# Attention and a maxout FFN on one core: seven visits for three head groups instead of nine, and FFN pieces in the score slots

## The chip, the cores and the metric

One core of one Trainium2 chip. (In this kernel TensorE does the matmuls, VectorE and ScalarE the elementwise work; PSUM is the memory that the matmuls write, and a "piece" or an AV holds banks of it until VectorE or ScalarE has read them.) The metric is the device time of one execution in microseconds (us). Most executions of a kernel agree within 0.3%. Ratios are the mean time of one kernel's fast runs over that of the other's fast runs of the same rounds, so they are not quite the ratios of the medians that stand beside them.

## The reference, cut to what matters

```python
def _attn_ref(q, k, v):                 # 8 batches, 12 heads, 448 tokens, 64 per head
    scores = scale * np.matmul(q, k.transpose(0, 1, 3, 2))
    m = np.max(scores, axis=-1, keepdims=True)
    e = np.exp(scores - m)
    attn = e / (np.sum(e, axis=-1, keepdims=True) + np.exp(-m) + 1e-09)
    return np.matmul(attn, v)

def _moe_ref(x, w1, w2, w3, w_out):     # 3584 tokens, 768 wide
    h = np.maximum(np.maximum(x @ w1, x @ w2), x @ w3)
    return h @ w_out
```

The attention's output, with the heads of a token side by side, is the FFN's `x`.

## The kernel before

The 96 heads are worked in 24 groups of four. A group's scores are seven units. A unit is four matmuls of 64x64 weights and 448 columns ("corners"), one for each quarter of the array, into one slot of two PSUM banks; ScalarE takes the exponential of a slot in one instruction. Then the weighted sum with V ("AV") is done for each of the two pairs of heads: 26 small matmuls (64x64 weights, 65 columns) and 18 wide ones (128x128, 65 columns). TensorE's time between is filled with pieces of the FFN: an up piece is six matmuls of 448 columns into one bank, an output piece six of 384.

The kernel works with eight banks of PSUM: three slots of two, and two single banks for the FFN. An AV takes a slot, so a visit has room for two units and an AV, or three units and no AV: three visits per group.

```python
ps_s = ctx.enter_context(tc.tile_pool(name="ps_s", bufs=3, space=bass.MemoryType.PSUM))
ps_b = ctx.enter_context(tc.tile_pool(name="ps_b", bufs=2, space=bass.MemoryType.PSUM))
...
visits = ((0, 1), (2, 3), (4, 5, 6))
...
for i in range(3, NI):
    ...
    for vi, units in enumerate(visits):
        n = 3 * i + vi
        scores(i, ej, units)                      # corners, then the exponentials
        ...
        if vi < 2:
            finish = av(i - 1, pj, vi, "E" if first else "EO")
        if n in adds:
            add_batch(adds[n])                    # a batch of FFN work becomes available
        per = STEP if first and vi < 2 else share(n)
        if finish:
            one()                                 # one FFN piece, then the rest of the AV
            finish()
        ...
        fill(per)                                 # FFN pieces, banks in turn
```

The last tile of an AV (the 64 tokens that are left of 448 after three tiles of 128, for both heads of the pair) is summed in two banks, so ScalarE copies one half and VectorE adds the other (`finish`): one copy, an add, a reciprocal and two scaled copies for each pair.

The softmax here doesn't subtract the row's maximum and nothing guards it: scores larger than these inputs give would overflow.

Of the kernel before, what the change touches and what calls it, by code (L numbers as in the profile page):

```python
# [17 lines left out]
LAMBDA = 256.0  # L18


@with_exitstack
def kernel(
# [36 lines left out]
    LAST = 6  # L59
# [10 lines left out]
    ps_s = ctx.enter_context(tc.tile_pool(name="ps_s", bufs=3, space=bass.MemoryType.PSUM))  # L70
    ps_b = ctx.enter_context(tc.tile_pool(name="ps_b", bufs=2, space=bass.MemoryType.PSUM))

    ctx.enter_context(tc.manual_schedule())

# [97 lines left out]
    def warm(n, cols=512):  # L172
        ps = ps_b.tile([128, 512], FP32, tag="b", name="warm")
        for _ in range(n):
            nc.tensor.matmul(
                out=ps[:, 0:cols], lhsT=wz[:, 0:128], rhs=wz[:, 0:cols], start=True, stop=True
            )
# [14 lines left out]
    def transpose_pe(i, pr, pool, k_eng, q_engs):  # L192


        def tile_of():
            if pool is ps_s:
                return ps_s.tile([128, 2, 1024], MMDT, tag="s", name="trT")[:, 0]
            return ps_b.tile([128, 1024], MMDT, tag="b", name="trT")

        kr, qr = raw[i]["k"], raw[i]["q"]  # L200
        kj = (0, 1, 2) if pr == 0 else (3, 4, 5, 6)
        qt = (-1, 1, 3, 5, 0, 2, 4) if pr == 0 else (6, 8, 10, 12, 7, 9, 11, 13)
        n = -(-len(qt) // len(q_engs))
        jobs = [(k_eng, "k", kj[0], kr, [2 * b for b in kj])]
        for e, eng in enumerate(q_engs):
            jobs.append((eng, "q", pr * 7 + e * n, qr, qt[e * n : (e + 1) * n]))
        if i not in KT:
            KT[i] = att_pool.tile([P, T * 128], MMDT, tag="KT", name="KT")
            QT[i] = att_pool.tile([P, (NB + 1) * 128], MMDT, tag="QT", name="QT")
        tps = [tile_of() for _ in jobs]  # L210
        for tp, (eng, nm, o, src, toks) in zip(tps, jobs):
            for j, t in enumerate(toks):
                nc.tensor.transpose(
                    out=tp[:, ts(j, 128)],
                    in_=src[:, t + 1 : t + 3, :].rearrange("x t d -> x (t d)"),
                    identity=ident16,
                )
        for tp, (eng, nm, o, src, toks) in zip(tps, jobs):
            dst = {"k": KT, "q": QT}[nm][i]
            evac(eng, dst[:, o * 128 : (o + len(toks)) * 128], tp[:, 0 : len(toks) * 128])  # L220

    def transpose_once(i, nm, eng):
# [4 lines left out]
        tp = ps_b.tile([128, 1024], MMDT, tag="b", name="trT")  # L227
# [62 lines left out]
    def scores(i, ej, units, part="EO"):  # L290
# [5 lines left out]
        for n in range(0, len(units), per):  # L296
            us = units[n : n + per]
            stp = ps_s.tile([128, 2, 512], FP32, tag="s", name="stp")
# [35 lines left out]
    def av_tail(i, ej, pr, ws=(0, 1, 2, 3)):  # L334

        eF, vt = e_buf[ej], vt_buf[i % NV]
        ps = ps_s.tile([128, 2, 512], FP32, tag="s", name="avp")
# [15 lines left out]
    def av_last(i, ej, pr):  # L353



        eF, vx, vt = e_buf[ej], v_buf[i % NV], vt_buf[i % NV]
        ps = avs[i, pr]

        def tile_mm(r, hh, o, rhs, stop):  # L360
            nc.tensor.matmul(  # L361
                out=ps[hh * HP : hh * HP + HP, r, 3 * D1 : 4 * D1],
                lhsT=eF[r * HP : r * HP + HP, o : o + HP],
                rhs=rhs,
                start=False,
                stop=stop,
                skip_group_check=True,
            )

        n = where[pr, None, TL]  # L370
        for hh in range(2):
            tile_mm(hh, hh, e_col(n, 3), vt[hh * HP : hh * HP + HP, pr, 0:D1], False)
        for c, x in enumerate((X1, X3, X2)):
            for r in range(2):
                for hh in range(2):
                    o = e_col(where[pr, hh, x], 3)
                    rhs = vx[r * HP : r * HP + HP, 2 * pr + hh, x[0], 0:D1]
                    tile_mm(r, hh, o, rhs, c == 2)

    def av_main(i, ej, pr, ws=(0, 1, 2, 3), last=False):  # L380
# [29 lines left out]
        if not last:  # L410
            return None
        end = small.tile([P, D1], FP32, tag="end", name="end")
        rl = small.tile([P, 1], FP32, tag="rl", name="rl")
        nc.scalar.activation(out=end, in_=ps[:, 1, 3 * D1 : 4 * D1], func=AF.Copy)  # L414

        def finish():
            nc.vector.tensor_tensor(out=end, in0=ps[:, 0, 3 * D1 : 4 * D1], in1=end, op=ALU.add)
            nc.vector.tensor_scalar(
                out=rl, in0=end[:, D:], scalar1=1.0 / LAMBDA, scalar2=None, op0=ALU.add
            )  # L420
            nc.vector.reciprocal(out=rl, in_=rl)  # L421
            for hh in range(2):
                h = slice(hh * HP, hh * HP + HP)
                nc.scalar.activation(  # L424
                    out=xn[i][0:HP, pr, 3, hh], in_=end[h, 0:D], func=AF.Copy, scale=rl[h]
                )

        return finish
# [14 lines left out]
    def x_transpose_pe(i, part):  # L443
# [3 lines left out]
        tp = ps_b.tile([128, NP, 2, 128], MMDT, tag="b", name="xtp")  # L447
# [10 lines left out]
    def x_transpose_all(i):  # L458
        b, g = groups[i]
        tp = ps_b.tile([128, NP, 4, 128], MMDT, tag="b", name="xtp")  # L460
# [20 lines left out]
    def up_piece(b, fcs, i, q0, qn):  # L481
# [5 lines left out]
        p_i = ps_b.tile([128, 512], FP32, tag="b", name="p_i")  # L487
# [18 lines left out]
    def out_piece(bp, t, c, w, queues):  # L506
# [5 lines left out]
        op_ps = ps_b.tile([128, 512], FP32, tag="b", name="op_ps")  # L512
# [33 lines left out]
    def add_out(b):  # L546
        sy, sc = nc.sync, nc.scalar
        for t in range(0, 3) if b % 2 == 0 else range(3, 7):
            cuts = [(0, NW, None), (NW, NW, (sy, sy))]
            if b == B - 1 and t == 6:  # L550
                cuts = [(0, NW, (sy, sy)), (NW, 256, (sc, sc)), (NW + 256, 128, (sy, sc))]
# [9 lines left out]
    def fill(cols):  # L561
        credit[0] += cols
        while pieces and credit[0] > 0:
            f, a, w = pieces.pop(0)
            f(*a)
            credit[0] -= w
        if not pieces:
            credit[0] = min(credit[0], 0.0)

    def one():  # L570
        if pieces:
            fill(max(0.0, 1.0 - credit[0]))
# [9 lines left out]
    def av(i, ej, pr, part):  # L582
        if i >= LAST:
            av_tail(i, ej, pr, (0, 1, 2))
            av_last(i, ej, pr)
            return av_main(i, ej, pr, (0, 1, 2), True)
# [24 lines left out]
    transpose_pe(0, 0, ps_s, DV, (AC, DV))  # L611
    attend("O", 0, S01)
    transpose_pe(0, 1, ps_b, DV, (DV,))
    attend("O", 0, S23, S46)
    warm(4)
    transpose_pe(1, 0, ps_b, AC, (DV,))
    transpose_pe(1, 1, ps_s, AC, (DV,))
# [5 lines left out]
    transpose_pe(2, 0, ps_b, AC, (DV,))  # L623
    transpose_pe(2, 1, ps_s, AC, (DV,))
# [34 lines left out]
    visits = ((0, 1), (2, 3), (4, 5, 6))  # L659
    adds = {3 * (3 * b + 4) + (b >= PE_X): b for b in range(1, B - 1)}  # L660
# [3 lines left out]
    def share(n):  # L664


        nxt = min([a for a in adds if a > n], default=3 * NI + 2)
        rest = range(n, nxt)
        sums = [AVC if m % 3 < 2 and m < 3 * NI else 0 for m in rest]
# [8 lines left out]
    for i in range(3, NI):  # L678
        ej, pj = (i + 1) % NEB, i % NEB
        first = i == 3  # L680
        if PE_QK <= i + 2 < NI:
            transpose_dma(i + 2)
        if first:
            load_v(i + 2)
        for vi, units in enumerate(visits):
            n = 3 * i + vi
            scores(i, ej, units)
            if i == 4 and vi == 0:
                prep_v(i, DV)
            finish = None  # L690
            if vi < 2:
                finish = av(i - 1, pj, vi, "E" if first else "EO")
            if n in adds:
                add_batch(adds[n])
            per = STEP if first and vi < 2 else share(n)
            if finish:
                one()
                finish()
            if vi == 1 and i > 3 * PE_X:
                x_transpose_dma(i - 1)  # L700
            if vi == 0 and first:
                x_transpose_pe(1, "E")
            if vi == 2 and first:
                x_transpose_pe(i - 1, "E")
                fill(per / 2)
                prep_v(i, DV)
                for w, cols in ((0, (0, NE)), (1, (0, NE)), (2, (NE, NO)), (2, (0, NE))):
                    add_up(0, *cols, [(w, f) for f in (0, 2, 4)])
                add_out(0)
                per = share(n)  # L710
            if vi == 2 and 3 < i <= 3 * PE_X:
                x_transpose_all(i - 1)
            if first:
                fill(per)
                per = 0
            if i + 1 < PE_QK and vi < 2:
                transpose_once(i + 1, "qk"[vi], (AC, DV)[vi])
            fill(per)
        if i + 1 < PE_QK:
            shift_q(i + 1, nc.gpsimd)  # L720
        if first:
            load_qk(i + 3)
        if i < 5:
            load_more(i + 3, i + 4)
        if 5 <= i + 1 < NI:
            prep_v(i + 1, nc.gpsimd)
        if PE_QK <= i + 2 < NI:
            shift_q(i + 2, nc.gpsimd)
        if i >= 5:
            load_more(i + 3, i + 4)  # L730

    for pr in range(NP):
        finish = av(NI - 1, NI % NEB, pr, "EO")
        one()
        finish()
    x_transpose_dma(NI - 1)
# [33 lines left out]
```

## Time and profile before

| | before |
|---|---|
| median of 3 runs | 338.42 us (338.1 to 339.23) |
| span of the profiled run | 336.9 us |
| TensorE, VectorE, ScalarE busy | 97%, 59%, 54% |
| FFN matmul of 448 columns, start to start | 189 ns |
| attention block of a visit with AV (two units) | 1.30 us |
| attention block of a visit without (three units) | 0.69 us |

The busy shares come from the top of the profile's page. The last three rows come from the starts of single matmuls in the trace: the block runs from the first score matmul to the first FFN matmul. TensorE is the bound and hardly waits, so the question is only how many nanoseconds of attention lie between the FFN pieces. The lines that carry this are shown in the prediction.

### The profile page before, as it was taken

To read this page: it belongs to the slowest core of one execution; us is meant where nothing else is said; L and a number is where in the kernel's file an instruction comes from. 1 tells how busy PE (TensorE), PEld (TensorE's weight loads), DVE (VectorE), ACT (ScalarE), POOL (GpSimd) and SP (SyncE) were. 2 spreads that over 40 slices of the span, in tenths; PEclk is the share of its full clock that TensorE was granted. 3 is DMA by queue.
4 is the path that set the end of the run, shared out by engine and by line. 5 is a ranking of instruction groups with operands and counts; after the bars stand their busy time and mean duration, and the time that the engine had idled before them with its cause. 6 is when DMAs were issued, how large, how long until landed. Compare 5 with 4: busy or idle time off the path is not lost.

```text
span 336.9 us, 10248 instructions
## 1 busy us (share of the span) xinstructions
PE 326.1 (97%) x4316; PEld 195.9 (58%) x4316; DVE 199.9 (59%) x521; ACT 183.1 (54%) x289; POOL 146.7 (44%) x260
## 2 busy tenths in 40 slices
PE   7899999999999999999999999999999999999993
PEld 3668788866556655565546646555556555565552
DVE  4556675566566556556656556556556556575552
ACT  4768856655665755676556655666565665420000
POOL 8596578880671539170854328351754000000000
PEclk9999999999999999999999999999999999999999
DMA  8999999799799999969996999989990730124016
GB/s 141 197 200 207 203 205 191 128 161 191 109 108 132 171 234 145 124 96 190 177 156 81 114 259 120 150 99 220 186 149 18 164 89 2 31 47 129 0 33 157
DMA packets 84815, 46.46 MB, mean 138 GB/s; under 512 B 53280, under 2 KB 81312, under 8 KB 84768
## 3 DMA queue, kind: packets, MB, share of 16 engines
q0 software_dynamic: 29120, 21.80, 48.6%
q1 hardware_dynamic: 55264, 23.60, 41.3%
q8 instruction: 34, 0.56, 0.7%
q10 hardware_dynamic: 384, 0.39, 0.4%
q14 instruction: 13, 0.11, 0.1%
HBM read 44.04 MB, written 11.01 MB: 163 GB/s over the span
## 4 chain that ended last, share of the span: by engine, by line
PE 87%; DMA 5%; ACT 2%; DVE 2%; issue 1%; POOL 1%; POOLq 0%; ACTq 0%
PE p_i L490 48%; PE op_ps L514 14%; PE stp L304 11%; PE avp L388 9%; DMA xT<-xn 3%; ACT e L324 2%; DMA ld_q<-in_q_dram 2%; PE avp L344 2%; PE avp L361 1%; DVE xn L404 1%; PE trT L229 1%; DVE QT L190 1%; PE xtp L463 0%; ACT QT L188 0%; DVE rb L401 0%
## 5 line engine op out<-in xcount | busy, mean ns | idle before, releaser
L324 ACT ACTIVATE e<-stp 128x896 f16<-128x896 f32 (+4 forms) x171 | 143.9, 901 | 60.3 <-PE stp L304 60.1
L490 PE MATMUL p_i<-xT,w 128*128 128x448 f16 (+2 forms) x972 | 173.1, 332 | 0.5 <-DMA xT<-xn 0.3
L490 PEld LDWEIGHTS <-w 128*128 128x128 f16 x972 | 90.2, 98 | 69.1 <-issue 6.0
L249 POOL COPY QT<-QT 64x384 f16<-64x384 f16 (+1 forms) x84 | 46.9, 558 | 93.9 <-DMA QT<-ld_q 69.2
L501 DVE TENSOR_TENSOR hT<-hT,p_i 128x448 f16<-128x448 f16 (+2 forms) x96 | 59.7, 622 | 35.7 <-PE p_i L490 35.6
L514 PE MATMUL op_ps<-w,hT 128*128 128x384 f16 (+2 forms) x342 | 58.5, 323 | 0.0
L304 PE MATMUL stp<-QT,KT 64*64 64x448 f16 (+2 forms) x756 | 48.1, 338 | 2.6 <-ACT e L324 0.9
L499 DVE CAST hT<-p_i 128x448 f16<-128x448 f32 (+2 forms) x48 | 30.0, 625 | 25.2 <-PE p_i L490 25.2
L514 PEld LDWEIGHTS <-hT 128*128 128x128 f16 x342 | 32.0, 98 | 22.4 <-issue 2.0
L424 ACT ACTIVATE xn<-end,rl 64x64 f16<-64x64 f32 x72 | 24.9, 346 | 34.5 <-DVE rl L421 34.1
L521 DVE TENSOR_SCALAR o_sb<-op_ps 128x384 f32<-128x384 f32 (+2 forms) x57 | 31.2, 547 | 17.4 <-PE op_ps L514 16.8
L388 PE MATMUL avp<-vx,e 128*128 128x65 f16 x936 | 38.6, 194 | 0.0
L388 PEld LDWEIGHTS <-e 128*128 128x128 f16 x936 | 32.1, 97 | 2.3
L304 PEld LDWEIGHTS <-KT 64*64 64x64 f16 x756 | 15.8, 105 | 26.8 <-issue 23.9
L398 DVE TENSOR_SCALAR rb<-avp 128x6 f32<-128x6 f32 (+2 forms) x54 | 8.8, 164 | 36.8 <-PE avp L388 36.8
L404 DVE TENSOR_TENSOR xn<-avp,rb 128x384 f16<-128x384 f32 (+2 forms) x54 | 29.3, 543 | 1.8
L433 POOL COPY vx<-ld_v 128x768 f16<-128x768 f16 x21 | 17.2, 820 | 6.8 <-issue 4.2
L344 PEld LDWEIGHTS <-e 64*64 64x64 f16 x624 | 13.7, 107 | 8.1 <-issue 1.7
L102 POOL DMA_DIRECT2D ld_q<-in_q_dram x24 | 17.4, 723 | 2.3 <-DMA w<-in_moe_w_dram 1.1
L102 POOL DMA_DIRECT2D ld_k<-in_k_dram x24 | 17.3, 722 | 2.1 <-DMA w<-in_moe_w_out_dram 1.1
L414 ACT ACTIVATE end<-avp 128x65 f32<-128x65 f32 x36 | 8.2, 227 | 17.1 <-PE p_i L490 12.4
L115 POOL DMA_DIRECT2D ld_v<-in_v_dram x24 | 15.2, 634 | 2.6 <-DMA w<-in_moe_w_dram 1.3
(52 smaller groups left out, 162.1 us busy)
## 6 DMA issues: line engine op xcount, KB each, us to landing
out_dram<-o_sb SPq DMA_DIRECT2D x54, 192.0 KB, 4.0
ld_v<-in_v_dram POOLq DMA_DIRECT2D x48, 128.0 KB, 5.1
ld_k<-in_k_dram POOLq DMA_DIRECT2D x23, 224.0 KB, 6.6
ld_q<-in_q_dram POOLq DMA_DIRECT2D x23, 224.0 KB, 7.5
w<-in_moe_w_dram POOLq DMA_DIRECT2D x9, 384.0 KB, 9.2
w<-in_moe_w_out_dram POOLq DMA_DIRECT2D x3, 384.0 KB, 8.5
xT<-xn SPq DMA_TRANSPOSE x18, 4.8
QT<-ld_q SPq DMA_TRANSPOSE x17, 7.3
```

Source lines behind the costliest of these rows:

```text
L102: nc.gpsimd.dma_start(out=tiles[nm][:, 1 : NP * T + 1].rearrange("x (r t) d -> x r (t d)", r=NP)[:, p0:p1], in_=src[:, p0:p1],)
L249: eng.tensor_copy(out=t[d0 : d0 + HP, o * 128 : (o + n) * 128], in_=t[s0 : s0 + HP, a * 128 : (a + n) * 128],)
L304: nc.tensor.matmul(out=stp[half * HP : half * HP + HP, par, j * qn : (j + 1) * qn], lhsT=k_block(i, pr, h2, x[half]), rhs=q_cols(i, pr, h2 ...
L324: nc.scalar.activation(out=dst, in_=src, func=AF.Exp, scale=scale)
L388: nc.tensor.matmul(out=ps[:, hh, j * D1 : (j + 1) * D1], lhsT=eF[:, o : o + 128], rhs=vx[:, 2 * pr + hh, (x[0]), 0:D1], start=False, stop= ...
L404: nc.vector.tensor_tensor(out=xn[i][:, pr, ws[0] : ws[0] + nw].rearrange("p j h d -> p h j d"), in0=acc[:, :, :, 0:D], in1=rb.unsqueeze(3) ...
L424: nc.scalar.activation(out=xn[i][0:HP, pr, 3, hh], in_=end[h, 0:D], func=AF.Copy, scale=rl[h])
L490: nc.tensor.matmul(out=p_i[:, j * qn : (j + 1) * qn], lhsT=w_sb[i][:, dc, ts(fc, 128)], rhs=xT[b][:, dc, q0 : q0 + qn], start=(dc == 0), s ...
L499: nc.vector.tensor_copy(out=dst, in_=src)
L501: nc.vector.tensor_tensor(out=dst, in0=dst, in1=src, op=ALU.max)
L514: nc.tensor.matmul(out=op_ps[:, 0:w], lhsT=hT[bp][:, fc, ts(t, 128)], rhs=wout_sb[:, fc, c : c + w], start=(fc == 0), stop=(fc == NFC - 1),)
L521: nc.vector.tensor_scalar(out=o_sb[:, c : c + w], in0=op_ps[:, 0:w], scalar1=1.0 / LAMBDA, scalar2=None, op0=ALU.mult,)
```

## The change

The intent: three units in every visit, also beside an AV. For that the AV is packed into one bank (7 x 65 = 455 columns of 512) instead of a slot, and its small tiles run in the quarters of the array that a unit's corners leave free: the first unit's two "anti" corners go together with 14 small tiles on the diagonal quarters, and the last unit's diagonal corners with 12 small tiles on the anti ones. Three groups then need seven visits. As the AV holds one of the two single banks, the FFN pieces go into score slots whose exponentials are done, and only the last piece of a visit into the remaining bank. The code makes the second lot of small tiles wait for the first by way of a no-op on ScalarE (the prediction gives the reason). Further, the last tile of an AV needs no add any more, and the last output tile is stored in two parts instead of three, each by two queues.

```diff
-    ps_s = ctx.enter_context(tc.tile_pool(name="ps_s", bufs=3, space=bass.MemoryType.PSUM))
-    ps_b = ctx.enter_context(tc.tile_pool(name="ps_b", bufs=2, space=bass.MemoryType.PSUM))
+    slots = [ps.tile([128, 2, 512], FP32, name=f"ps{j}") for j in range(3)]
+    banks = [ps.tile([128, 512], FP32, name=f"pb{j}") for j in range(2)]
...
+    def visit(units, pair):
...
+        ps = banks[0]
...
+        def turn_over(mm):
+            turned = nc.scalar.nop()
+            tc.add_manual_dep(turned.ins, mm.ins.name, AFTER, reason="PSUM bank")
+            return turned
...
+            (s0, _), (s1, _), (s2, _) = qk
+            for at in anti:
+                s0(*at)
+            turned = turn_over(smalls(diag, True))
+            for s, at in ((s0, diag), (s1, anti), (s1, diag), (s2, anti), (s2, diag)):
+                for corner in at:
+                    s(*corner)
+            smalls(anti, False, turned)
+            for _, power in qk:
+                power()
+            wides()
...
+    def places(cols, pair):
...
+        mid = [] if pair else [banks[0]]
+        while len(mid) < n:
+            mid.append(slots[(turn["s"] + len(mid) - (not pair)) % 3][:, 0])
+        ahead.extend(mid[: max(n - 1, 0)] + [banks[1]] * (n > 0))
...
-                cuts = [(0, NW, (sy, sy)), (NW, 256, (sc, sc)), (NW + 256, 128, (sy, sc))]
+                cuts = [(0, NW, None), (NW, 256, (sy, sc)), (NW + 256, 128, (sy, sc))]
...
+    ONE = 6
+    for g in range(ONE, NI, 3):
+        todo = [(g + n // 7, n % 7) for n in range(21)]
+        for n in range(7):
+            us = todo[3 * n : 3 * n + 3]
...
+        if n == NV0 + 2:
+            ahead.append(banks[0])
+            x_transpose_all(ONE - 1)
```

## The prediction

> **What bounds the kernel now.** I read the page first (busy shares), then the waits of TensorE, then the chain of waits in a steady stretch, then single starts in the trace.
>
> ```profile
> PE 326.1 (97%) x4316; PEld 195.9 (58%) x4316; DVE 199.9 (59%) x521; ACT 183.1 (54%) x289; POOL 146.7 (44%) x260
> ...
> PE 87%; DMA 5%; ACT 2%; DVE 2%; issue 1%; POOL 1%; POOLq 0%; ACTq 0%
> PE p_i L490 48%; PE op_ps L514 14%; PE stp L304 11%; PE avp L388 9%; DMA xT<-xn 3%; ACT e L324 2%; DMA ld_q<-in_q_dram 2%; PE avp L344 2%; PE avp L361 1%; DVE xn L404 1%; PE trT L229 1%; DVE QT L190 1%; PE xtp L463 0%; ACT QT L188 0%; DVE rb L401 0%
> ```
>
> TensorE is the chain (87%); no other engine is over 59% busy. 97% busy does not by itself say that TensorE is used well, so the next question is whether it waits and what it streams.
>
> ```profile
> PE stp L304 <- ACT e L324: 0.9, 3, 0.4
> PE p_i L490 <- DMA xT<-xn: 0.3, 1, 0.3
> ```
>
> TensorE's waits add up to some 5 us, nearly all in the start-up; from 76 us on there is one, for a transposing DMA. So only work or switches taken off TensorE shorten the middle. The chain of waits from 201.9 to 212 us, groups of work in order (start, us, what):
>
> ```profile
> 201.97 0.50 PE stp L304 x8
> 202.47 0.09 PE avp L344 x12
> 202.56 0.13 PE avp L361 x14
> 202.69 0.67 PE avp L388 x18
> 203.36 3.40 PE p_i L490 x18
> ...
> 211.56 0.69 PE stp L304 x12
> ```
>
> The 18 FFN matmuls take 3.40/18 = 189 ns each, 448 columns at 2.4 GHz plus 2 ns: at the rate of the array, nothing to win. What can shrink is the attention block of each visit. From starts in the trace: a visit with two score units and one AV takes 1.30 us from its first score to the first FFN matmul, a visit with three units and no AV 0.69 us, and the last FFN matmul before each is followed after 283 instead of 189 ns (0.094 us more). So 1.394 and 0.784 us. Inside: a score phase of four 64x64 corners is 0.189 us (the first 0.213), the 26 small AV matmuls go in rounds of four, one round per 32 ns, the 18 wide ones 32 ns each (0.58 us in all), and between the last small and the first wide lie 0.128 us instead of 0.03.
>
> **What the Trainium skill says.** "TensorEngine Tiling (Array Packing)", section Key Properties: changing the tiling mode drains TensorE, and different tiles can load weights and multiply in parallel. The trace agrees: the two switches of a visit are the extra 0.094 and 0.10 us above, and the four corners start 3 to 4 ns apart. The same page, Gotcha 1: different row tiles cannot write the same PSUM bank at the same time. The kernel before always gives its two row tiles two banks, so its trace shows nothing on it. "PSUM — Partial Sum Buffer", section The four PSUM rules: only the first matmul in a bank and quadrant may carry the clearing flag, later groups there must come after it; that is why the change makes its second half of small tiles wait. "TensorE: Matmul & The Clock Gate", Part 3, The mechanism: matmuls start and end in strict order; the starts in the trace do.
>
> **The change part by part.** The order of instructions of the changed kernel: up to group 5 nearly as before; then visits of three units each, 2 corners of the first unit, 14 small AV tiles, 10 corners, 12 small tiles, 18 wide, then 3 to 5 FFN pieces. 42 visits (37 with an AV, 5 without) and one last AV stand where 18 groups had 54 visits and two last AVs.
>
> Before, from the first score of group 6 (65.85 us) to 297.1 us: group 6, with AVs of the older form, 2x1.39 + 0.69 + 0.46 (its eight transposes) + 3x0.094 = 4.2; 34 x 1.394 = 47.4; 17 x 0.784 = 13.3; the last two AVs 0.92 + 0.93 + 2x0.094 = 2.0; the one DMA wait 0.46 (646 instead of 189 ns). Sum 67.4 us. All else there is FFN matmuls, the same before and after.
>
> After, one visit with AV: two score corners use two of the four tiles, and 7 rounds of two small tiles (7x32 = 0.224) use the other two; then the second half of unit 0 starts at about 0.23, and the two pairs of tiles run staggered, phases of 0.189: the last corners start at 0.61, beside them 6 rounds of small tiles until 0.79. Wide tiles start after the 0.1 drain, at 0.90, and take 0.58: FFN could start at 1.48; with the 0.094 in front 1.57 us. 37 x 1.574 = 58.2; 5 x 0.784 = 3.9; eight transposes 0.46; the last AV alone, whose two halves hide behind nothing, 0.224 + 0.13 + 0.58 + 0.1 + 0.19 + 0.13 + 0.094 = 1.45. Sum 64.1. Visits alone save 3.3 us with the DMA wait counted.
>
> Small parts:
> - The x of group 5 goes into the bank that the next AV needs first: about 0.2 to the end of the last transpose, 0.65 for the copy out, less the 0.15 until the small tiles want it: +0.7 us, once. It was on TensorE before as well (eight transposes each for groups 3, 4 and 5), so nothing else changes.
> - ACT loses 36x0.227 + 72x0.346 = 33 us of 183, VectorE some 36x(0.22 + 0.15 + 0.16) = 19 us and gains 72 small multiplies (estimate 0.2 each, 14 us). Neither was waited for: worth nothing by itself.
> - The end. Last matmul at 331.4, last eviction done 331.93, yet the last SP issue starts only at 333.51, behind two longer ones; its landing at about 335.6 sets the end. Six issues in 331.3 to 334.0 are 0.44 us each; four from 331.65 end at about 333.5. I take -0.6 us.
>
> So without a new wait: -3.3 + 0.7 - 0.6 = -3.2, i.e. 335.2 us.
>
> **The rivals.**
> 1. The first FFN piece waits for the exponential. It now goes into the slot of unit 0. In the trace an exponential starts 0.425 us after the start of its last corner, takes 0.913 to 0.917 us, and a release takes another 0.04. The last corner of unit 0 starts at 0.23 instead of 0.01, so the slot is free at 0.23 + 0.425 + 0.917 + 0.04 = 1.61, against 1.48 when TensorE would be ready: 0.13 to 0.14 us in 36 visits, +5.0 us, and 340.2. For: every duration is from this trace. Against: two sums of 1.5 us are subtracted, each good to perhaps 0.1; and whoever chose this slot probably looked for that wait. The later pieces do not wait: the second exponential ends 0.81 later, a piece takes 1.13.
> 2. The small tiles don't overlap with the corners, or the two row tiles in one bank are served in turn (gotcha above): up to 0.2 us more in each half, 37 x 0.2 to 0.4 = +7 to +15 us, 343 to 352. Against: the corners and small tiles of before do run four abreast; the different lengths side by side and one bank for two row tiles are new, though the two write different partitions.
> 3. The wait through ScalarE is late. The last diagonal tile ends at 0.38 (start 0.19 plus 0.19), two releases of 0.05 and a no-op bring 0.50 to 0.55, and the tiles are due at 0.61. It just fits; 0.05 late would be +2 us in all.
> 4. The last x transposing DMA: 3.1 us to landing when the queues are quiet (300.13 us). The change leaves 4 x 0.975 + 4 x 0.189 + 0.1 = 4.75 us of matmuls to hide it and about 1.5 us of VectorE in front: 4.6 in all. 0 to 0.5 us.
>
> **Range and chances.** Half of rival 1 between 335.2 and 340.2 gives 337.7; I say 337.7, near the time before. The whole attention block is 67.4 us and the tiles' own streaming bounds what packing can save: even without any wait the gain is about 1%, so faster by over 2% (under 331.7) needs something I don't see: 0.04. Slower by over 2% (over 345.2) needs rival 2, or 1 and 3 together and large: 0.08. Within 2%: 0.88. Range 333.6 to 342.0.
>
> **What would show it.** Right: first score to first FFN matmul between 1.5 and 1.65 us in AV visits; small tiles starting some 32 ns apart per round between the corners; about 0.9 us from the first score to the first wide tile; the last SP issue before 333.5 relative to the same end of matmuls. Rival 1 shows as a wait of the FFN's TensorE line on ACT e, about 0.14 us in most visits. Rival 2 shows as a first wide tile later than 1.1 us after the first score. Rival 3 shows as a wait of the second small-tile group on ScalarE. I would be wrong if the visits' own time fell below 1.5 us, which would mean that small and large tiles overlap better than their tiles' occupancy allows.

## The result, and the profile after

The changed kernel takes 346.03 us (median of 4, 345.76 to 346.37) against 338.26 us of before: ratio 1.0226, 95% interval 1.0201 to 1.0252. It is 2.3% slower, outside the range of 333.6 to 342.0. Executions over 1.5% slower than the fastest of the same kernel are left out of the means.

The top of the page of the changed kernel:

```profile
PE 331.3 (96%) x4324; PEld 203.8 (59%) x4324; DVE 203.2 (59%) x489; ACT 149.9 (44%) x181; POOL 146.5 (43%) x260
```

ScalarE lost 33 us as foreseen; TensorE is busy for about the same share as before (96 against 97%), which is 5 us more. Busy shares do not tell what happened. I cut both traces at three points: the first FFN matmul of 448 columns (batch 1 begins), the first matmul of the last batch, and the last matmul's start.

| stage (us) | before | after | difference |
|---|---|---|---|
| start to batch 1 | 77.21 | 81.96 | +4.75 |
| middle, to the last batch | 225.75 | 228.15 | +2.40 |
| last batch | 28.42 | 28.42 | 0.00 |
| tail, from the last matmul's start | 5.50 | 5.94 | +0.44 |
| span | 336.88 | 344.47 | +7.59 |

The first two rows have to be read together: at the start of batch 1 the changed kernel has done three units and one AV more (a visit's worth), so part of the 4.75 us is work pulled forward. The 2.40 us after it are then more of a loss than they look.

TensorE's waits in the changed kernel that the kernel before does not have, less one of 0.2 us in the start-up (wait, then us in total, times, longest). In all these lines `ps` is a score slot, `pb` a single bank, `e` the exponentials, `xn` the attention's output and `xT` its transpose, `o_sb` an output piece:

```profile
PE pb L594 <- DVE o_sb L625: 0.6, 1, 0.6
PE pb L452 <- DVE xT L573: 0.4, 1, 0.4
PE pb L452 <- DVE xn L523: 0.3, 1, 0.3
PE ps L594 <- ACT e L425: 0.3, 1, 0.3
PE pb L567 <- DVE xn L523: 0.2, 1, 0.2
```

Five small waits, 1.8 us together: this view does not explain 7.6 us either. It counts only time in which no matmul is in flight. Each wide AV matmul is shown 193 ns long though the next could start 32 ns after it, so a wait of up to some 160 ns behind it is covered by its own tail and appears as busy time. Only the starts show it. TensorE in one visit of the changed kernel (start us, us, line, out<-in, shapes, number):

```profile
200.81 0.38 PE L414 MATMUL ps<-QT,KT 64*64 64x448 f16 x2
200.82 0.31 PE L452 MATMUL pb<-vt,e 64*64 64x65 f16 x8
200.97 0.23 PE L452 MATMUL pb<-vx,e 64*64 64x65 f16 x4
201.02 0.35 PE L414 MATMUL ps<-QT,KT 64*64 64x448 f16 x2
201.03 0.20 PE L452 MATMUL pb<-vx,e 64*64 64x65 f16 x2
201.06 0.55 PE L414 MATMUL ps<-QT,KT 64*64 64x448 f16 x6
201.41 0.22 PE L452 MATMUL pb<-vt,e 64*64 64x65 f16 x2
201.44 0.35 PE L414 MATMUL ps<-QT,KT 64*64 64x448 f16 x2
...
201.73 0.74 PE L481 MATMUL pb<-vx,e 128*128 128x65 f16 x18
202.45 2.24 PE L594 MATMUL ps<-xT,w 128*128 128x448 f16 x11
```

and ScalarE in the same stretch:

```profile
201.49 2.54 ACT L425 ACTIVATE e<-ps 128x896 f16<-128x896 f32 x3 [2.60 <-PE ps L414]
```

Small tiles (L452) and corners (L414) do run beside each other, and the first wide tile (L481) starts 0.92 us after the first corner: both as predicted (0.90). But the first FFN matmul (L594) comes at 202.45, 1.643 us after the first corner, where 1.48 was possible. The last wide tile is followed after 179 ns instead of 33 (in 32 of the 33 long visits the step is 179 to 189 ns, in one 459). The first exponential begins at 201.49 (0.675 us after the first corner) and lasts 0.917 us: it ends at 1.592, and the FFN piece that was put into its slot starts 0.051 us later. That is rival 1, in full.

The early visits of the new form show a second loss. TensorE and VectorE in the second of them:

```profile
69.34 1.14 PE L618 MATMUL pb<-w,hT 128*128 128x384 f16 x6
70.41 0.38 PE L414 MATMUL ps<-QT,KT 64*64 64x448 f16 x2
71.08 0.31 PE L452 MATMUL pb<-vt,e 64*64 64x65 f16 x8 [0.29 <-DVE xn L523]
```

```profile
69.54 0.17 DVE L508 TENSOR_SCALAR rb<-pb 128x7 f32<-128x7 f32 x1 [1.02 <-PE pb L481]
69.74 0.20 DVE L511 RECIPROCAL rb<-rb 128x7 f32<-128x7 f32 x1
69.98 0.56 DVE L513 TENSOR_TENSOR xn<-pb,rb 128x384 f16<-128x384 f32 x1
70.45 0.57 DVE L523 TENSOR_SCALAR xn<-pb,rb 64x64 f16<-64x64 f32 x2
```

An AV's bank is free again when the two multiplies of L523 end, 1.68 us after the next FFN piece began. With a single output piece (1.07 us) in the visit, the next AV's small tiles stand 0.67 us behind the corners. In the next visits the same step is 0.30 and 0.78 us (the last behind the copy of the x of group 5, which used the AV's bank), and the eight transposes come 0.4 us late (a step of 559 ns, where 162 is usual). Just before these visits an output piece also waits for VectorE's `hT` (a step of 457 instead of 162 ns). In long visits there is no such wait.

Third, at the last batch (TensorE, then VectorE):

```profile
308.33 1.14 PE L618 MATMUL pb<-w,hT 128*128 128x384 f16 x6
310.11 0.73 PE L594 MATMUL pb<-xT,w 128*128 128x448 f16 x3 [0.65 <-DVE o_sb L625]
```

```profile
309.50 0.56 DVE L625 TENSOR_SCALAR o_sb<-pb 128x384 f32<-128x384 f32 x1 [0.42 <-PE pb L618]
```

The first up piece takes the bank of the output piece just before it, by the order of banks in the built program, and waits for its eviction: the step between two matmuls is 975 instead of 162 ns.

### The profile page after: what moved, and what is told of

Same layout as the page of the kernel before. It is cut to its first block, busy times and chain, and to the rows that moved or that the text cites. A ratio compares the mean times of both kernels' runs of the same rounds, so it can differ in the third digit from the quotient of the medians.

```text
span 344.5 us, 10309 instructions
## 1 busy us (share of the span) xinstructions
PE 331.3 (96%) x4324; PEld 203.8 (59%) x4324; DVE 203.2 (59%) x489; ACT 149.9 (44%) x181; POOL 146.5 (43%) x260
## 4 chain that ended last, share of the span: by engine, by line
PE 89%; DVE 3%; ACT 2%; DMA 2%; issue 1%; POOL 1%; DVEq 0%; POOLq 0%; ACTq 0%
PE ps L594 28%; PE pb L594 21%; PE ps L618 8%; PE pb L618 8%; PE pb L481 7%; PE ps L414 7%; PE pb L452 4%; PE ps L379 2%; PE ps L322 2%; DMA ld_q<-in_q_dram 2%; ACT e L342 1%; PE ps L362 1%; DVE xn L395 1%; DVE QT L210 1%; PE pb L247 1%
## 5 line engine op out<-in xcount | busy, mean ns | idle before, releaser
L425 ACT ACTIVATE e<-ps 128x896 f16<-128x896 f32 x126 | 106.5, 917 | 126.5 <-PE ps L414 109.7
L594 PEld LDWEIGHTS <-w 128*128 128x128 f16 x972 | 92.8, 98 | 69.6 <-issue 2.7
L594 PE MATMUL ps<-xT,w 128*128 128x448 f16 x480 | 96.3, 352 | 0.3 <-ACT e L425 0.3
L594 PE MATMUL pb<-xT,w 128*128 128x448 f16 (+2 forms) x492 | 80.4, 312 | 1.0 <-DVE o_sb L625 0.6
L605 DVE TENSOR_TENSOR hT<-hT,ps 128x448 f16<-128x448 f16 x59 | 36.7, 622 | 13.7 <-PE ps L594 12.5
L342 ACT ACTIVATE e<-ps 128x896 f16<-128x896 f32 (+4 forms) x45 | 36.4, 869 | 18.4 <-PE ps L322 18.2
L414 PE MATMUL ps<-QT,KT 64*64 64x448 f16 x504 | 40.9, 354 | 0.0
L618 PE MATMUL pb<-w,hT 128*128 128x384 f16 (+2 forms) x180 | 32.7, 321 | 0.1
L605 DVE TENSOR_TENSOR hT<-hT,pb 128x448 f16<-128x448 f16 (+2 forms) x37 | 23.0, 621 | 16.5 <-PE pb L594 16.3
L618 PE MATMUL ps<-w,hT 128*128 128x384 f16 x162 | 28.9, 326 | 0.0
L481 PE MATMUL pb<-vx,e 128*128 128x65 f16 x684 | 28.0, 194 | 0.0
L414 PEld LDWEIGHTS <-KT 64*64 64x64 f16 x504 | 16.8, 105 | 17.6 <-issue 14.2
L481 PEld LDWEIGHTS <-e 128*128 128x128 f16 x684 | 23.3, 97 | 2.0
L452 PEld LDWEIGHTS <-e 64*64 64x64 f16 x988 | 21.6, 107 | 3.3 <-issue 1.6
L452 PE MATMUL pb<-vt,e 64*64 64x65 f16 x532 | 22.5, 198 | 0.7 <-DVE xT L573 0.4
L523 DVE TENSOR_SCALAR xn<-pb,rb 64x64 f16<-64x64 f32 x76 | 21.2, 279 | 0.5
```

What stands on the lines that cost most here:

```text
L342: nc.scalar.activation(out=dst, in_=src, func=AF.Exp, scale=scale)
L414: return nc.tensor.matmul(out=stp[half * HP : half * HP + HP, par, 0:S], lhsT=k_block(i, pr, h2, x[half]), rhs=q_cols(i, pr, h2, par, "EO" ...
L425: nc.scalar.activation(out=dst, in_=stp[:, :, 0:S], func=AF.Exp, scale=scale)
L452: yield lambda m=m, w=w, o=o, rhs=rhs: nc.tensor.matmul(out=ps[cc, w * D1 : (w + 1) * D1], lhsT=eF[rr, o : o + HP], rhs=rhs, start=start a ...
L481: nc.tensor.matmul(out=ps[:, (3 * hh + j) * D1 : (3 * hh + j + 1) * D1], lhsT=eF[:, o : o + 128], rhs=vx[:, 2 * pr + hh, (x[0]), 0:D1], st ...
L523: nc.vector.tensor_scalar(out=dst[0:HP, pr, 3, hh], in0=acc[h, 6, 0:D], scalar1=rb[h, 6:7], scalar2=None, op0=ALU.mult,)
```

## The experiments

My theory then: (a) the slot wait, about 0.15 us in most visits, some 5 us; (b) the AV's bank in the short early visits, some 1.5 us; (c) the bank collision, 0.8 us; (d) perhaps the large last store, 0.4 us. Its rivals: wide tiles or the drain end the visit rather than the slot; ScalarE is the bound in the short visits; small tiles and corners gain nothing from running together.

Nine kernels were run, in three jobs, each beside the kernel before on the same chip. All results were correct. Whole times suffer from the spread of the kernel before (337.8 to 341.7 us in the first job), so I read the stages too. In the new form the middle repeats to 0.01 us where it is not touched (228.15 twice, 221.89 twice); between the kernel before and e5_before_newtail, which do the same there, it differs by 0.27 us:

| run | median us | ratio to before (95%) | to batch 1 | middle | tail |
|---|---|---|---|---|---|
| changed kernel | 346.03 | 1.0226 (1.0201 to 1.0252) | 81.96 | 228.15 | 5.94 |
| e1_split | 348.00 | 1.0257 (1.0208 to 1.0306) | 82.12 | 229.90 | 5.95 |
| e2_oldtail | 346.29 | 1.0215 (1.0164 to 1.0266) | 82.39 | 228.15 | 5.60 |
| e3_bank | 345.40 | 1.0178 (1.0120 to 1.0236) | 81.83 | 227.34 | 6.03 |
| e4_smalls_after | 362.92 | 1.0699 (1.0648 to 1.0750) | 82.54 | 244.28 | 6.08 |
| e5_before_newtail | 338.04 | 0.9984 (0.9947 to 1.0021) | 76.82 | 226.02 | 5.16 |
| e6_freebank | 340.24 | 1.0037 (1.0007 to 1.0068) | 81.67 | 222.75 | 5.47 |
| e7_early | 343.99 | 1.0135 (1.0108 to 1.0163) | 80.57 | 227.35 | 6.02 |
| e8_all | 338.51 | 0.9977 (0.9955 to 0.9999) | 80.40 | 221.89 | 6.31 |
| e10_all_newtail | 338.41 | 0.9979 (0.9952 to 1.0006) | 80.26 | 221.89 | 5.96 |

### e1_split: the first exponential in two halves

```diff
-                nc.scalar.activation(out=dst, in_=stp[:, :, 0:S], func=AF.Exp, scale=scale)
+                cuts = ((0, 1), (1, 2)) if not qk_first and pair else ((0, 2),)
+                for a, z in cuts:
+                    nc.scalar.activation(
+                        out=dst[:, a:z], in_=stp[:, a:z, 0:S], func=AF.Exp, scale=scale
+                    )
```

> The changed kernel with the exponential of a visit's first unit in two instructions, one for each of its two banks, so that the bank of the first FFN piece comes free sooner. Theory A (the first FFN piece waits for the exponential of unit 0, about 0.15 us in 32 to 36 visits): first score to first FFN matmul goes from 1.643 to about 1.50 us, the last wide tile is again followed after about 33 instead of 183 ns, and the whole is 4.5 to 5.3 us faster than the changed kernel, about 341 us. Rival B (the visit is long because the wide tiles end late or the array drains, not because of the slot): 1.64 stays and the time stays at 346 us or grows a little, as ScalarE has one more instruction a visit.

It was slower: the middle grew from 228.15 to 229.90 us. By my own words that speaks for rival B, but the trace says otherwise:

ScalarE:

```profile
202.41 1.79 ACT L427 ACTIVATE e<-ps 128x448 f16<-128x448 f32 x3 [2.60 <-PE ps L414]
```

TensorE, the first FFN piece of the same visit:

```profile
203.44 0.73 PE L598 MATMUL ps<-xT,w 128*128 128x448 f16 x3
```

From this visit's first corner the halves start at 0.675 and 1.115 us, the second ends at 1.653, and the FFN matmul starts at 1.704: again 0.051 us after the end of what it waits for. In the trace the first half updates no semaphore, only the second does, and the FFN piece waits for that one. So the edit did not free the bank: it made the same wait 0.06 us longer in each visit, and the time followed. That is evidence for the slot wait, but only by a correlation, so e6 was needed.

### e2_oldtail: the last tile stored as before

```diff
-                cuts = [(0, NW, None), (NW, 256, (sy, sc)), (NW + 256, 128, (sy, sc))]
+                cuts = [(0, NW, (sy, sy)), (NW, 256, (sc, sc)), (NW + 256, 128, (sy, sc))]
```

> The changed kernel with the last tile stored as before, in three parts. In the traces the end of the changed kernel, from its last matmul, is 0.45 us longer than that of before, though its last store is issued 0.56 us sooner: theory: one large store lands later than two small ones, so this run is 0.4 to 0.6 us faster, about 345.5 us. Rival (my prediction): the new tail saves time and this run is 0.6 us slower, 346.6 us.

346.29 us, no difference; the tail in its one trace is 0.34 us shorter. Inconclusive by itself, see e5 and e10.

### e3_bank: no collision at the last batch

```diff
     fill(float("inf"))
+    turn["b"] = 0
     add_batch(B - 1)
```

> The changed kernel with the turn of the two FFN banks set so that the first piece of the last batch does not take the bank of the piece just before it. Theory: the 975 ns step at 309 us (0.81 us over the usual 162) is that bank's eviction and goes away: 0.8 us faster, 345.2 us. Rival: the last transposing DMA of x lands hardly sooner, so the wait moves from the bank to the DMA in the same piece and under 0.3 us is won.

The middle went from 228.15 to 227.34 us, 0.81 us less, and the wait on `o_sb` is gone from TensorE's waits; nothing took its place. Cause (c) is shown in the trace. The whole time (345.40) agrees, though its interval overlaps that of the changed kernel.

### e4_smalls_after: nothing interleaved

```diff
             (s0, _), (s1, _), (s2, _) = qk
-            for at in anti:
-                s0(*at)
-            turned = turn_over(smalls(diag, True))
-            for s, at in ((s0, diag), (s1, anti), (s1, diag), (s2, anti), (s2, diag)):
-                for corner in at:
-                    s(*corner)
+            for s, _ in qk:
+                for corner in anti + diag:
+                    s(*corner)
+            turned = turn_over(smalls(diag, True))
             smalls(anti, False, turned)
```

> The changed kernel with all twelve corners first and both groups of small tiles after them, nothing interleaved. If small tiles and corners truly overlap in the changed kernel: here the first wide tile starts at about 1.45 instead of 0.92 us, first score to first FFN matmul is about 2.05 us, and the exponential of unit 0 is done by then; 36 x 0.4 = 14 us slower, about 360 us. If the overlap was worth nothing (served in turn): no more than 2 us of difference.

362.92 us, 17 us slower than the changed kernel (expected 14). The first wide tile starts at 1.40 us (expected 1.45), the FFN at 2.13. So the interleaving is worth about 0.48 us a visit at the wide tiles, and my rival 2 of the prediction is out. Not all of it is overlap of matmuls: here the second lot starts 301 ns after the last small tile of the first, where a round takes 32 ns, so some 0.27 us of the 0.48 is the wait for the no-op, which the corners cover in the changed kernel; that leaves about 0.2 us for running side by side. One part of the expectation missed: I said that the exponential would be done by then. TensorE and ScalarE of one visit:

```profile
204.07 0.76 PE L414 MATMUL ps<-QT,KT 64*64 64x448 f16 x12
204.67 0.29 PE L452 MATMUL pb<-vt,e 64*64 64x65 f16 x8
```

```profile
205.24 2.54 ACT L425 ACTIVATE e<-ps 128x896 f16<-128x896 f32 x3 [3.87 <-PE pb L452]
```

The first unit's corners had all been started by 204.09, but ScalarE began only at 205.24 and its releaser is a small tile (`pb L452`), not a corner. In ScalarE's program the no-op that orders the two lots of small tiles stands before the exponentials. It starts at 205.10, 0.23 us after the last small tile of the first lot, and the exponential 0.14 us after it: it had to wait for the small tiles. The FFN piece again starts 0.051 us after the exponential's end (2.082 and 2.133 us).

### e6_freebank: the first FFN piece in the bank that is free

The last piece of the visit before is evicted well before the first piece of this one. So the remaining single bank can serve twice: for the first piece and again for the last, and the slots take only the pieces between.

```diff
-        mid = [] if pair else [banks[0]]
-        while len(mid) < n:
-            mid.append(slots[(turn["s"] + len(mid) - (not pair)) % 3][:, 0])
+        mid = [banks[1]] * (n > 2) if pair else [banks[0]]
+        k = len(mid)
+        while len(mid) < n:
+            mid.append(slots[(turn["s"] + len(mid) - k) % 3][:, 0])
```

> The changed kernel with the first FFN piece of a visit in the bank that the last piece of the visit before left (evicted by then), the next ones in the score slots: nothing new waits for the exponential of unit 0. Splitting that exponential did not free the slot (the piece then started 0.051 us after the end of the second half, as it did after the whole before). Theory A (the slot wait): first score to first FFN matmul becomes 1.49 to 1.52 us where a visit has three pieces or more, the middle stage goes from 228.15 to about 223.8 us, and the whole is 4 to 5 us faster, about 341.5 us. Rival (the wide tiles or the drain end the visit): 1.64 stays. Rival 2: the bank is not evicted in time by VectorE and the wait moves there, first or last piece.

340.24 us. The middle fell by 5.40 us, to 222.75 us (expected 223.8). TensorE in one visit, and ScalarE:

```profile
197.62 0.38 PE L414 MATMUL ps<-QT,KT 64*64 64x448 f16 x2
...
198.53 0.74 PE L481 MATMUL pb<-vx,e 128*128 128x65 f16 x18
199.11 1.30 PE L594 MATMUL pb<-xT,w 128*128 128x448 f16 x6
200.24 0.54 PE L594 MATMUL ps<-xT,w 128*128 128x448 f16 x2
```

```profile
198.29 2.54 ACT L425 ACTIVATE e<-ps 128x896 f16<-128x896 f32 x3 [2.45 <-PE ps L414]
```

Everything up to the wide tiles is as in the changed kernel, and the exponential starts at the same 0.67 us. Only the piece's output is now `pb` instead of `ps`, and it starts at 199.11, 1.49 us after the first corner, 33 ns behind the last wide tile. The second piece, in the slot, starts at 200.24 without waiting. Cause (a) is shown: it is the slot wait that cost 5.4 us, and neither the drain nor the wide tiles. Rival 2 of this run (the bank is not evicted in time) did not appear.

### e7_early: the short early visits

```diff
-        if n >= NV0 and places(per, pair) < 2 and finish:
+        if NV0 - 1 <= n < NV0 + 3:
+            per = (1.0 if n < NV0 else 12 * (NW + 6) - 1.0) - credit[0]
...
+        if n >= NV0 and (places(per, pair) < 2 or n < NV0 + 3) and finish:
...
-            ahead.append(banks[0])
+            ahead.append(slots[(turn["s"] + 2) % 3][:, 0])
             x_transpose_all(ONE - 1)
```

> The changed kernel with two output pieces in each of its first three visits of the new form, their AV's last tile copied out at once (before the evictions), and the x of group 5 transposed into a score slot instead of the AV bank. Theory: the AV bank has no second buffer, and in short visits the next AV waits for VectorE to read it (steps of 0.67, 0.30 and 0.78 us and 0.3 before the transposes); here these go, the first stage ends about 1.5 us sooner. By chance the banks' parity also changes, so the 0.8 us of the last batch go as well: about 343.7 us in all. Rival: ScalarE with three exponentials in visits of 2.6 us is the bound there, and then the waits turn into waits for ACT e and less than 0.5 us is won in the first stage.

343.99 us; batch 1 begins at 80.57 instead of 81.96 us (1.4 us sooner, expected 1.5), and the waits of the AV's bank on `xn` and `xT` are gone from TensorE's waits, with no wait on ACT e in their place in that stretch. Cause (b) is shown: the changed kernel and the two that share its early visits wholly (e2, e3) reach batch 1 at 81.83 to 82.39 us, the three with this edit at 80.26 to 80.57. A part is the wait for `hT`, as the edit moves that output piece too. And the early visits are not free of waits. TensorE, then VectorE, in this run:

```profile
69.43 1.14 PE L618 MATMUL pb<-w,hT 128*128 128x384 f16 x6
70.70 0.38 PE L414 MATMUL ps<-QT,KT 64*64 64x448 f16 x2
```

```profile
70.09 0.56 DVE L625 TENSOR_SCALAR o_sb<-ps 128x384 f32<-128x384 f32 x1
```

The first corner now waits for VectorE to empty the slot of the output piece (458 ns after the last FFN matmul instead of 256), a later corner stands 0.2 us behind the copy of the x of group 5, and the first output piece of three of these visits again waits for the exponential (a step of 109 to 181 ns instead of 33). From one FFN matmul to the next, the four visits still take about 1.3 us more than the prediction's 1.574 us each and 0.46 us for the transposes. The middle is 0.80 us shorter because the parity of the banks changed too, as said before the run.

### e5_before_newtail: the new storing alone, on the kernel before

> The kernel before with only the new storing of the last tile. From the last matmul to the end: 5.50 us before, 5.94 to 6.08 us in four kernels with the new tail, 5.60 with the old one put back. Theory (the large last store lands late): 5.9 to 6.1 us here, the whole 0.4 us slower than before. Rival: the tail's length comes with the other part of the change, and stays at 5.5 us.

338.04 us, ratio 0.9984: no difference, and the tail is 5.16 us, shorter than before. My theory (d) fails: I expected 5.9 to 6.1 us.

### e8_all and e10_all_newtail: the repairs together

All of e3, e6 and e7, with the old tail (e8) and with the new one (e10).

> All repairs together: first piece in the free bank, early visits, the last batch's bank, the old tail. If the four causes are independent the gains add up: 4.5 + 1.5 + 0.8 + 0.4 = 7.2 us less than the changed kernel, about 338.8 us, the same as the kernel before within 0.5%. If they hide each other, 341 us or more.

> The three repairs of the first job that worked (free bank for the first piece, early visits, the last batch's bank), with the new storing of the last tile kept. The tail has been 5.16 to 6.31 us in eight executions, with no order by old or new tail, so my theory of the late large store is probably noise: then this run has the same time as the run with all repairs and the old tail (338.5 us, ratio 0.998 to before) within 0.5 us. If the new tail does cost 0.4 us: 339 us. Whether this version beats the kernel before: at most by 0.5%, 336.8 to 338.8 us.

338.51 and 338.41 us. The gains add up: 346.03 less 5.4, 1.4 and 0.8 us is 338.4. Against the kernel before the ratios are 0.9977 (0.9955 to 0.9999) and 0.9979 (0.9952 to 1.0006): 0.2% faster by the mean and at most 0.5%, the same for all practical purposes. The tail with the old storing is now 6.31 us, the longest of all, and with the new one 5.96: the tail differs from execution to execution by more than the two ways of storing differ, and what the new storing is worth stays open.

## Why the prediction was wrong

Right, by its own steps:
- The block of a visit without a new wait. Predicted: first wide tile at 0.90, FFN at 1.48 us. Measured: 0.92, and 1.49 in e6_freebank.
- The bound on the gain. Predicted: about 1% even without any wait. With all repairs the kernel gains 0.2%. As a bound it holds; as a sum it was too good (below).
- Rival 2 is out (e4_smalls_after). (Its upper end should have been 350, not 352 us: 335.2 and 14.8.)
- Rival 3 "just fits", as written: in the long visits the second lot of small tiles starts 67 or 68 ns after the no-op and 198 ns after the corner before it in its quarter; where the no-op comes earlier (three early visits) that step is 189 ns. So it is late by some 9 ns, no more. The second lot starts 0.601 us after the first corner, where 0.61 was predicted.
- Rival 4 did not show either: with the bank collision gone (e3_bank), nothing waits for the last DMA of x.

Wrong (the first four points decided it):
- **The weight on rival 1.** The prediction had this wait worked out from the trace, 0.13 to 0.14 us in 36 visits, 5.0 us, and then took half of it, because "two sums of 1.5 us are subtracted" and because "whoever chose this slot probably looked for that wait". The runs show the whole of it: 0.15 us in 32 long visits, 0.43 in one, and 5.4 us in e6_freebank. Every term of the two sums was within 0.03 us of what the new trace shows (the last corner of unit 0 at 0.260 instead of 0.23, the exponential 0.415 instead of 0.425 us after it), so the subtraction was good. The guess about the author was no evidence. Written at full weight the prediction would have said 340.2 us, still 5.8 us short: the rest is in the next three points. "Slower by over 2% needs rival 2, or 1 and 3 together and large" failed with them.
- **Two waits missing from the list.** The AV's bank has no second buffer, which costs at least the 1.4 us that e7_early wins back in the short early visits (I had seen only the transposes' part, 0.7 us, which by single starts is 1.3 us), and two pieces in a row fall into one bank at the last batch, 0.8 us. Both could be read from the order of instructions and the tiles' names before any run: I checked the first piece and the x transposes of one visit for who reads a bank before, and not each change of pattern.
- **The sum without waits.** It was 335.2 us; the repaired kernel takes 338.4. From the first score of group 6 to the last batch e10_all_newtail saves 1.4 us (235.67 against 237.11), where 3.3 less 0.7, so 2.6, were foreseen; the four early visits, which I had counted as free of waits, keep about 1.3 us (e7_early). The first score of group 6 comes 0.62 us later, which I had not counted. And the tail is 0.46 us longer in these two traces instead of 0.6 shorter.
- **The tail.** The step taken was that the end follows the last store's issue. That issue did come sooner (1.57 us after the last matmul in the changed kernel, 2.13 before), but its landing took 3.4 us instead of 2.1, in that trace. Over all traces nothing of the gain can be seen (5.16 to 6.31 us, whatever the storing).
- **The order of matmuls.** The prediction says that matmuls keep strict order and that "the starts in the trace do". That was a misreading; nothing in the sum rests on it. In the kernel before, two of the small tiles of L361 with `vx` start 3 to 6 ns ahead of the second one with `vt`, which stands before them in the program.

Open: the start-up. From the first FFN matmul to the last 256-column one before group 6 both kernels of the old form take 43.1 us and all nine of the new form 43.6 to 43.9, so this is a loss and not spread. One wait that the nine have and the two do not is for VectorE's copy of a transposed K (a step of some 322 ns instead of 109); the rest I did not separate.

## What to carry to other kernels

When a buffer gets a new user, write down for each use who reads it last and when, in single starts, and do so at every change of the pattern (first, short and last rounds), not only in the steady state. A wait that comes out of measured durations goes into the prediction in full. On a pipelined engine a wait shorter than an instruction's shown length is invisible in busy shares and in lists of waits: compare the step from one start to the next with the same step where nothing is waited for.

## What the Trainium skill lacked or had wrong

- "Perfetto Trace Analysis", section Identifying the Most-Contended Engine, says that matmul busy time is a poor measure; it does not say that lists of waits share the fault. Here the list shows 0.3 us, of one visit, for a wait that cost 5.4 us: steps of 179 to 189 instead of 33 ns behind matmuls shown 193 ns long.
- "TensorE: Matmul & The Clock Gate", Part 3, The mechanism, says that matmuls start in strict program order. In the changed kernel two corners that stand after all 14 small tiles start at 213 and 218 ns, the last two of those small tiles at 223 and 227 ns: matmuls on other quarters of the array overtake by 5 to 14 ns there, and by some 30 ns where the second lot's first small tiles (601 and 604 ns) start before the last two corners (632 and 638). My prediction had repeated the page.
- "TensorEngine Tiling (Array Packing)", Gotcha 1, says that different row tiles cannot access one PSUM bank at the same time. Here two row tiles write one bank on different partitions in rounds of some 32 ns, as fast as into two banks before, and all results are correct; the limit, if it holds, is narrower than this page writes it. (The skill's "PSUM — Partial Sum Buffer", section PSUM bank collisions raise a hardware error, has the narrower form: it reports the error for one bank and one quadrant.)
- "TensorEngine Tiling (Array Packing)", section Key Properties, says that a change of tiling mode drains TensorE and gives no figure: 0.094 us from full to quarters and 0.10 us back in these traces.
- No page that I used tells what ordering two lots of matmuls through a no-op on another engine takes: here 374 ns from the start of the last matmul of the first lot to the start of the first of the second, and 301 ns in e4_smalls_after. It also holds up that engine's own queue: the exponential of e4_smalls_after started 1.17 us after the first corner, where 0.43 is an estimate from the last corner's start (0.01) and the 0.425 us that passed in the kernel before.
